# Two column parts of 64 in the sums and results of an attention kernel, with transposes, rows and banks of a piece in another order

## The chip, the core and the metric

The kernel runs on one core of one Trainium2 chip. The metric is the time of one execution on the device in microseconds (us). Three runs of the kernel before took 1344.69, 1345.78 and 1349.05 us; the median, 1345.78, stands for it. The profile is of one more execution, which took 1344.1 us. Engines are named as in the profile: PE is TensorE (PEld its weight loads), DVE is VectorE, ACT is ScalarE, POOL is GpSimd, SP is SyncE.

## The reference

Three layers follow one another on 8 batches of 576 positions. The first is attention with exponential features, for 8 heads of 64 channels:

```
phi(x)  = concat(exp(p - m), exp(-(p - m))),  p = x @ w_phi (64 x 128),  m = max|p| over the row
kv, z   = phi(k)^T v,  sum of phi(k) over the positions
out     = phi(q) kv / (phi(q) z + 1e-6)
```

The second mixes each position with the one before it by `mu_k` and `mu_r`, and computes `sigmoid(xr @ w_r) * (relu(xk @ w_k)^2 @ w_v)` with a hidden size of 1024. The third computes `h = relu(x @ w_in)`, a convolution of three taps over the positions, and `(h * sigmoid(conv)) @ w_out`. All data is float32.

## The kernel before, in words

The attention is cut into 32 pieces: a batch and a pair of its heads. Pieces 0 to 5 go through `attention`, an older path that this change leaves as it is. From piece 6 (`SW`) on, `block(Pi)` does one piece and prepares the next two:

- `turn` (L478): transposes on TensorE. `px` is the normalised result `xn` of the piece before, which ScalarE copies into `xT`, the input of the second layer; `pt` are the centred query projections of the two heads, which ScalarE turns into the features `qf` (L510); `pr` holds the last 64 positions of both (L500, L504).
- `rows_last`, `rows4` (L424, L433): projections of keys (`pk`, of piece Pi + 2) and queries (`pq`, of piece Pi + 1) and of the last positions (`p1`, listed as `p`), through L422. VectorE takes the maximum and centres (L441, L442).
- `sums4` (L466): `pkv`, the products of key features with values, of piece Pi + 1. Each product has 128 columns and is cut into column parts of 32, which write 32 partitions each (L474).
- `results` (L513): `pn`, the query features times `kvf`, of piece Pi, cut in the same way (L522); VectorE divides (L524 to L530).
- `features` (L451): ScalarE's exponentials for the keys of piece Pi + 2.

A float32 matmul in the program is two on the chip, so a product of four parts is eight matmuls and eight weight loads. The profile counts those of the chip.

The second layer ("expert work", `psk`, `psr`, `psv` through `mm3`, L143 to L145) is a generator `m`. `feed` takes steps from it between the blocks, so TensorE does a block, then 84 to 192 expert matmuls, then the next block. From piece 6 on TensorE's order is that of the program (`manual_schedule`); the order of the other engines is set by a scheduler that simulates the program. After the last piece (847 us) the rest of the second layer and the whole third layer follow, without attention beside them.

PSUM has eight banks. Three belong to the pool `psm` (tag "mm"), which the expert work uses too, and five to `psa` (tag "at"). Each pool hands its banks out in turn. A block takes three of "mm" and ten of "at", so a tile waits for the readers of the tile that had its bank three, or five, tiles earlier.

`bridge` (L535) stands between the two paths. It prepares piece 7 and then calls `run_late` (L368), which brings the last result of the older path into `xT`: two matmuls `pr` (L361) that need `rr`, four small rows that a DMA writes (L349).

Of the kernel before, what the change touches and what calls it, by code (L numbers as in the profile page):

```python
# [45 lines left out]
def fused_kernel(ctx: ExitStack, tc: tile.TileContext, qk, va, wphi, ones2, mu, wk, wv, wr, win, wout, cw, out):  # L46
# [103 lines left out]
    with ExitStack() as p1:  # L150
# [217 lines left out]
        def run_late():  # L368
            for l_ in late:
                l_()  # L370
            late.clear()
# [50 lines left out]
                T.matmul(o, x[r, j * P:j * P + P], wp0[r, h * FT:h * FT + FT], start=True, stop=True)  # L422

        def rows_last(Pi):  # L424
            ps = [psm.tile([P, 512], F32, tag="mm", name="p1"), psa.tile([P, 512], F32, tag="at", name="p1")]
            ps = [p_[:, :FT].rearrange("p (a n) -> p a n", a=1) for p_ in ps]
            rows(Pi, [(ps[h][:, 0], h, 4) for h in range(2)])
            t = pool.tile([P, 1, 2, FT], F32, tag="t1", bufs=2, name="t")
            for h in range(2):
                centre(ps[h], t[:, :, h])  # L430
            ts[Pi] = [t]

        def rows4(Pi, j0, nm):  # L433
            ps = [psa.tile([P, 4, FT], F32, tag="at", name=nm) for _ in range(2)]
            rows(Pi, [(ps[h][:, j], h, j0 + j) for j in range(4) for h in range(2)])
            return ps

# [28 lines left out]
        def sums4(Pi):  # L466

            kp, vt = kps_.pop(Pi), vts.pop(Pi)
            pkv = psa.tile([P, 2, 2, V1], F32, tag="at", name="pkv")
            prods = [(pkv[:, c, h], kp[h][:, i, c], vt[:, i, h]) for i in range(4) for h in range(2) for c in range(2)]  # L470
            prods += [(pkv[:, c], kp[2][:, c], vt[:, 4]) for c in range(2)]
            for i, (o, k_, v_) in enumerate(prods):
                for r in range(0, P, 32):
                    T.matmul(o[r:r + 32], k_[:, r:r + 32], v_, start=(i == 0), stop=(i == len(prods) - 1))  # L474
            kvs[Pi] = pool.tile([P, 2, 2, V1], F32, tag="kvh", bufs=2, name="kvf")
            A.copy(kvs[Pi], pkv)

        def turn(Pi):  # L478

            t1, *tq = ts[Pi]  # L480
            qf = [pool.tile([P, 2, S], F32, tag=("qh", "ql")[h], bufs=1, name="qf") for h in range(2)]
            if Pi - 1 in xns:
                xn = xns.pop(Pi - 1)
                px = psa.tile([P, 512], F32, tag="at", name="px")
                for j in range(4):
                    T.transpose(px[:, j * P:j * P + P], xn[:, j], ident)
            else:
                xn = None
            pr = psa.tile([P, 512], F32, tag="at", name="pr")
            if xn is not None:  # L490
                T.transpose(pr[:, :P], xn[:, 4], ident)
            for h in range(2):
                T.transpose(pr[:, P + h * P:2 * P + h * P], t1[:, 0, h], ident)
            if xn is not None:
                xt = main.tile([P, 2 + S], F32, tag="xT", bufs=XT, name="xT")
                G.memset(xt[:, 0:1], 0.0)
                A.copy(xt[:, 1:513], px)
                for h in range(2):
                    r = slice(64 * h, 64 * h + 64)
                    A.copy(xt[r, 513:577], pr[r, r])  # L500
                xT[divmod(Pi - 1, NP)] = xt
            for h in range(2):
                for c in range(2):
                    A.activation(qf[h][:, c, 512:], pr[:, P + h * P:P + h * P + 64], AF.Exp, scale=1.0 - 2 * c)  # L504
            for h in range(2):
                pt = psm.tile([P, 512], F32, tag="mm", name="pt")
                for j in range(4):
                    T.transpose(pt[:, j * P:j * P + P], tq[j // 2][:, j % 2, h] if Pi == SW else tq[h][:, j], ident)
                for c in range(2):
                    A.activation(qf[h][:, c, :512], pt, AF.Exp, scale=1.0 - 2 * c)  # L510
            return qf

        def results(Pi, qf):  # L513

            kv = kvs.pop(Pi)
            pn = [psa.tile([P, 512], F32, tag="at", name="pn")[:, :n * V1].rearrange("p (a n) -> p a n", n=V1) for n in (5, 4)]
            prods = [(0, 0, j, c) for j in range(4) for c in range(2)] + [(0, None, 4, c) for c in range(2)]
            prods += [(1, 1, j, c) for j in range(4) for c in range(2)]
            for b_, h, j, c in prods:
                for r in range(4):  # L520
                    h_, o = (r // 2, 512 + 32 * (r % 2)) if h is None else (h, j * P + 32 * r)
                    T.matmul(pn[b_][32 * r:32 * r + 32, j], qf[h_][:, c, o:o + 32], kv[:, c, h_], start=(j == 0 and c == 0), stop=(j == 4 - b_ and c == 1))  # L522
            rd = pool.tile([P, 9], F32, tag="rd4", bufs=2, name="rd")
            V.tensor_scalar(rd[:, :5], pn[0][:, :, D], 1e-6, None, ALU.add)  # L524
            V.tensor_scalar(rd[:, 5:], pn[1][:, :, D], 1e-6, None, ALU.add)
            V.reciprocal(rd, rd)
            xn = xns[Pi] = pool.tile([P, 5, P], F32, tag="xn", bufs=1, name="xn")
            for h in range(2):
                V.tensor_tensor(xn[:, :4, D * h:D * h + D], pn[h][:, :4, :D], rd[:, 5 * h:5 * h + 4].unsqueeze(2).to_broadcast([P, 4, D]), ALU.mult)
            V.tensor_scalar(xn[:, 4].rearrange("p (a n) -> p a n", a=2), pn[0][:, 4:5, :D].to_broadcast([P, 2, D]), rd[:, 4:5], None, ALU.mult)  # L530
            del ts[Pi]
# [3 lines left out]
        def bridge():  # L535

            rows_last(SW + 1)
            yield
            tk = centre4(rows4(SW + 1, 5, "pk"), "tk")
            load(SW + 2)  # L540
            yield
            features(SW + 1, tk)
            load_v(SW + 1)
            yield
            run_late()
            yield

        def block(Pi):

            nq, nk = Pi + 1 < B * NP, Pi + 2 < B * NP  # L550
            qf = turn(Pi)
            if nk:
                rows_last(Pi + 2)
                tk = centre4(rows4(Pi + 2, 5, "pk"), "tk")
            if nq:
                ts[Pi + 1] += centre4(rows4(Pi + 1, 0, "pq"), "tq")
                del xk[Pi + 1]
                sums4(Pi + 1)
            results(Pi, qf)
            if nk:  # L560
                features(Pi + 2, tk)
                load_v(Pi + 2)
            if Pi + 3 < B * NP:
                load(Pi + 3)

        def attention4(Pi):

            for n in range(NS):
                if n == 0:
                    while done[0] * NP <= Pi - 1 - XT:  # L570
                        next(m)
                    block(Pi)
                yield

        def mix(u, j):
# [280 lines left out]
```

## Time and profile before

| | |
|---|---|
| median of three runs | 1345.78 us |
| profiled execution, its span | 1344.1 us, 1342.3 us |
| TensorE busy | 1252.3 us (93%), 16,092 matmuls, as many weight loads |
| VectorE, ScalarE busy | 760.5 us (57%), 707.6 us (53%) |
| mean granted clock of TensorE | 0.985 of 2.4 GHz |
| pieces 6 to 31 | from 124 to 832 us |

In the 40 slices of the page TensorE shows 8 or 9 tenths busy up to about 800 us and 9 from there on. Its matmuls are pipelined: a row of the timeline gives the start of the first and the length up to the end of the last, and single matmuls in it overlap. A wait in brackets at the end of a row is the idle time before it and what ended it; "issue" means that nothing was waited for that the profile shows.

### The profile page before, as it was taken

To read this page: it belongs to the slowest core of one execution; us is meant where nothing else is said; L and a number is where in the kernel's file an instruction comes from. 1 tells how busy PE (TensorE), PEld (TensorE's weight loads), DVE (VectorE), ACT (ScalarE), POOL (GpSimd) and SP (SyncE) were. 2 spreads that over 40 slices of the span, in tenths; PEclk is the share of its full clock that TensorE was granted. 3 is DMA by queue.
4 is the path that set the end of the run, shared out by engine and by line. 5 is a ranking of instruction groups with operands and counts; after the bars stand their busy time and mean duration, and the time that the engine had idled before them with its cause. 6 is when DMAs were issued, how large, how long until landed. Compare 5 with 4: busy or idle time off the path is not lost.

```text
span 1342.3 us, 37269 instructions
## 1 busy us (share of the span) xinstructions
PE 1252.3 (93%) x16092; PEld 1216.9 (91%) x16092; DVE 760.5 (57%) x1457; ACT 707.6 (53%) x1654; POOL 137.7 (10%) x230
## 2 busy tenths in 40 slices
PE   8898899988898889898889999999999999999998
PEld 6687888988898889898888899999999999999998
DVE  7869654556556575465754553442754744744743
ACT  6877553545545455365553453442654654654653
POOL 6616300100001010010100000000000000000000
PEclk9998999989999999999999999999999999999999
DMA  7324212123222232222311100305012102112010
GB/s 252 108 57 131 92 34 64 53 83 100 70 79 85 69 103 81 79 85 70 100 59 47 38 21 20 144 19 179 24 49 72 36 37 71 33 39 71 26 46 36
DMA packets 56372, 96.13 MB, mean 72 GB/s; under 512 B 9100, under 2 KB 33808, under 8 KB 56208
## 3 DMA queue, kind: packets, MB, share of 16 engines
q1 hardware_dynamic: 42832, 65.89, 14.9%
q0 software_dynamic: 4528, 18.29, 4.5%
q10 hardware_dynamic: 8848, 9.57, 2.5%
q8 instruction: 126, 2.06, 0.6%
q14 instruction: 38, 0.31, 0.1%
HBM read 66.39 MB, written 27.26 MB: 70 GB/s over the span
## 4 chain that ended last, share of the span: by engine, by line
PE 85%; issue 6%; ACT 3%; DVE 3%; DMA 2%; POOL 1%; SPq 0%; DVEq 0%; ACTq 0%; POOLq 0%
PE psv L143 5%; PE psv L144 5%; PE psk L143 5%; PE psv L145 5%; PE psh L143 5%; PE psh L144 5%; PE pso L144 5%; PE pso L145 5%; PE psh L145 5%; PE pso L143 5%; PE psk L145 5%; PE psk L144 5%; PE pn L522 5%; PE pkv L474 4%; PE psr L143 2%
## 5 line engine op out<-in xcount | busy, mean ns | idle before, releaser
L143 PE MATMUL psv<-kh,wvl 128*128 128x288 f32 x512 | 154.3, 302 | 1.6 <-issue 1.6
L144 PE MATMUL psv<-kl,wvh 128*128 128x288 f32 x512 | 153.4, 300 | 1.7 <-issue 1.7
L143 PE MATMUL psk<-mh,wkl 128*128 128x288 f32 x512 | 154.9, 303 | 0.0
L145 PE MATMUL psk<-mh,wkh 128*128 128x288 f32 x512 | 152.3, 298 | 1.0 <-issue 1.0
L145 PE MATMUL psv<-kh,wvh 128*128 128x288 f32 x512 | 153.1, 299 | 0.1
L144 PE MATMUL psk<-ml,wkh 128*128 128x288 f32 x512 | 152.6, 298 | 0.0
L144 PE MATMUL psh<-xl,wih 128*128 128x288 f32 x512 | 151.1, 296 | 0.0
L143 PE MATMUL psh<-xh,wil 128*128 128x288 f32 x512 | 150.6, 296 | 0.0
L145 PE MATMUL psh<-xh,wih 128*128 128x288 f32 x512 | 150.1, 294 | 0.0
L626 ACT ACTIVATE kf<-psk 128x288 f32<-128x288 f32 x128 | 52.4, 410 | 184.7 <-PE psk L145 184.3
L144 PE MATMUL pso<-gl,woh 128*128 128x288 f32 x512 | 148.8, 295 | 0.0
L145 PE MATMUL pso<-gh,woh 128*128 128x288 f32 x512 | 148.7, 295 | 0.0
L143 PE MATMUL pso<-gh,wol 128*128 128x288 f32 x512 | 144.1, 293 | 0.0
L522 PE MATMUL pn<-kvf,qf 128*32 128x65 f32 x3744 | 70.4, 229 | 49.2 <-issue 47.4
L522 PEld LDWEIGHTS pn<-kvf,qf 128*32 128x32 f32 x3744 | 63.5, 114 | 54.2 <-issue 52.5
L760 DVE SCALAR_TENSOR_TENSOR ct<-h,cw,ct 128x576 f32<-128x576 f32 x64 | 52.4, 819 | 101.7 <-ACT ct L759 101.4
L143 PEld LDWEIGHTS psv<-kh,wvl 128*128 128x128 f32 x512 | 98.7, 193 | 3.2 <-issue 2.4
L144 PEld LDWEIGHTS psv<-kl,wvh 128*128 128x128 f32 x512 | 98.6, 193 | 1.9 <-issue 1.9
L143 PEld LDWEIGHTS psk<-mh,wkl 128*128 128x128 f32 x512 | 97.4, 191 | 2.8 <-issue 1.7
L69 POOL TENSOR_SCALAR hc<-hc 128x256 f32<-128x256 f32 (+1 forms) x53 | 60.1, 1137 | 379.8 <-ACT hc L68 301.0
L145 PEld LDWEIGHTS psv<-kh,wvh 128*128 128x128 f32 x512 | 98.5, 192 | 0.3 <-issue 0.3
L145 PEld LDWEIGHTS psk<-mh,wkh 128*128 128x128 f32 x512 | 97.9, 191 | 0.1
(145 smaller groups left out, 3159.6 us busy)
## 6 DMA issues: line engine op xcount, KB each, us to landing
rqk<-qk POOLq DMA_DIRECT2D x31, 576.0 KB, 4.5
va<-va SPq DMA_DIRECT2D x32, 325.0 KB, 4.2
x2s<-x SPq DMA_DIRECT2D x32, 288.0 KB, 2.3
x2r<-x2s ACTq DMA_DIRECT2D x32, 288.0 KB, 3.6
out<-ot SPq DMA_DIRECT2D x32, 288.0 KB, 2.1
raw<-wk SPq DMA_DIRECT2D x8, 512.0 KB, 5.7
raw<-wv SPq DMA_DIRECT2D x16, 256.0 KB, 2.7
raww<-win SPq DMA_DIRECT2D x16, 256.0 KB, 2.9
```

Of the source, the lines that this page charges most:

```text
L69: G.tensor_scalar(h, h, 2.0 ** -31, 122879.9921875 * 2.0 ** -16, ALU.max, ALU.min)
L143: T.matmul(ps, wl, xh, start=first, stop=False)
L144: T.matmul(ps, wh, xl, start=False, stop=False)
L145: T.matmul(ps, wh, xh, start=False, stop=last)
L474: T.matmul(o[r:r + 32], k_[:, r:r + 32], v_, start=(i == 0), stop=(i == len(prods) - 1))
L522: T.matmul(pn[b_][32 * r:32 * r + 32, j], qf[h_][:, c, o:o + 32], kv[:, c, h_], start=(j == 0 and c == 0), stop=(j == 4 - b_ and c == 1))
L626: A.activation(kf[:, j], ps, AF.Relu)
L760: V.scalar_tensor_tensor(t, h[:, 1:S + 1], cw0[:, fc, 1:2], t, ALU.mult, ALU.add)
```

## The change

`sums4` and `results` cut a product into two column parts of 64 where it was four of 32. `turn` transposes in the order `px`, `pt`, `pr` and takes `pt` from `psa`; ScalarE's copies out of `pr` come last. Both tiles of `rows_last` come from `psm`, and so does the second query tile of `rows4`. `run_late` leaves `bridge` and is called in `attention4` after the ninth of 15 steps of a piece (it has work in piece 6 alone).

```diff
@@ -422,7 +422,7 @@
                 T.matmul(o, x[r, j * P:j * P + P], wp0[r, h * FT:h * FT + FT], start=True, stop=True)
 
         def rows_last(Pi):
-            ps = [psm.tile([P, 512], F32, tag="mm", name="p1"), psa.tile([P, 512], F32, tag="at", name="p1")]
+            ps = [psm.tile([P, 512], F32, tag="mm", name="p1") for _ in range(2)]
             ps = [p_[:, :FT].rearrange("p (a n) -> p a n", a=1) for p_ in ps]
             rows(Pi, [(ps[h][:, 0], h, 4) for h in range(2)])
             t = pool.tile([P, 1, 2, FT], F32, tag="t1", bufs=2, name="t")
@@ -431,7 +431,8 @@
             ts[Pi] = [t]
 
         def rows4(Pi, j0, nm):
-            ps = [psa.tile([P, 4, FT], F32, tag="at", name=nm) for _ in range(2)]
+            ps = [psa.tile([P, 4, FT], F32, tag="at", name=nm)]
+            ps.append(psm.tile([P, 4, FT], F32, tag="mm", name=nm) if nm == "pq" else psa.tile([P, 4, FT], F32, tag="at", name=nm))
             rows(Pi, [(ps[h][:, j], h, j0 + j) for j in range(4) for h in range(2)])
             return ps
 
@@ -470,8 +471,8 @@
             prods = [(pkv[:, c, h], kp[h][:, i, c], vt[:, i, h]) for i in range(4) for h in range(2) for c in range(2)]
             prods += [(pkv[:, c], kp[2][:, c], vt[:, 4]) for c in range(2)]
             for i, (o, k_, v_) in enumerate(prods):
-                for r in range(0, P, 32):
-                    T.matmul(o[r:r + 32], k_[:, r:r + 32], v_, start=(i == 0), stop=(i == len(prods) - 1))
+                for r in range(0, P, 64):
+                    T.matmul(o[r:r + 64], k_[:, r:r + 64], v_, start=(i == 0), stop=(i == len(prods) - 1))
             kvs[Pi] = pool.tile([P, 2, 2, V1], F32, tag="kvh", bufs=2, name="kvf")
             A.copy(kvs[Pi], pkv)
 
@@ -479,35 +480,34 @@
 
             t1, *tq = ts[Pi]
             qf = [pool.tile([P, 2, S], F32, tag=("qh", "ql")[h], bufs=1, name="qf") for h in range(2)]
-            if Pi - 1 in xns:
+            old = Pi - 1 in xns
+            if old:
                 xn = xns.pop(Pi - 1)
+                xt = main.tile([P, 2 + S], F32, tag="xT", bufs=XT, name="xT")
+                xT[divmod(Pi - 1, NP)] = xt
+                G.memset(xt[:, 0:1], 0.0)
                 px = psa.tile([P, 512], F32, tag="at", name="px")
                 for j in range(4):
                     T.transpose(px[:, j * P:j * P + P], xn[:, j], ident)
-            else:
-                xn = None
-            pr = psa.tile([P, 512], F32, tag="at", name="pr")
-            if xn is not None:
-                T.transpose(pr[:, :P], xn[:, 4], ident)
-            for h in range(2):
-                T.transpose(pr[:, P + h * P:2 * P + h * P], t1[:, 0, h], ident)
-            if xn is not None:
-                xt = main.tile([P, 2 + S], F32, tag="xT", bufs=XT, name="xT")
-                G.memset(xt[:, 0:1], 0.0)
                 A.copy(xt[:, 1:513], px)
-                for h in range(2):
-                    r = slice(64 * h, 64 * h + 64)
-                    A.copy(xt[r, 513:577], pr[r, r])
-                xT[divmod(Pi - 1, NP)] = xt
-            for h in range(2):
-                for c in range(2):
-                    A.activation(qf[h][:, c, 512:], pr[:, P + h * P:P + h * P + 64], AF.Exp, scale=1.0 - 2 * c)
-            for h in range(2):
-                pt = psm.tile([P, 512], F32, tag="mm", name="pt")
+            for h in range(2):
+                pt = psa.tile([P, 512], F32, tag="at", name="pt")
                 for j in range(4):
                     T.transpose(pt[:, j * P:j * P + P], tq[j // 2][:, j % 2, h] if Pi == SW else tq[h][:, j], ident)
                 for c in range(2):
                     A.activation(qf[h][:, c, :512], pt, AF.Exp, scale=1.0 - 2 * c)
+            pr = psa.tile([P, 512], F32, tag="at", name="pr")
+            if old:
+                T.transpose(pr[:, :P], xn[:, 4], ident)
+            for h in range(2):
+                T.transpose(pr[:, P + h * P:2 * P + h * P], t1[:, 0, h], ident)
+            for h in range(2):
+                for c in range(2):
+                    A.activation(qf[h][:, c, 512:], pr[:, P + h * P:P + h * P + 64], AF.Exp, scale=1.0 - 2 * c)
+            if old:
+                for h in range(2):
+                    r = slice(64 * h, 64 * h + 64)
+                    A.copy(xt[r, 513:577], pr[r, r])
             return qf
 
         def results(Pi, qf):
@@ -517,9 +517,9 @@
             prods = [(0, 0, j, c) for j in range(4) for c in range(2)] + [(0, None, 4, c) for c in range(2)]
             prods += [(1, 1, j, c) for j in range(4) for c in range(2)]
             for b_, h, j, c in prods:
-                for r in range(4):
-                    h_, o = (r // 2, 512 + 32 * (r % 2)) if h is None else (h, j * P + 32 * r)
-                    T.matmul(pn[b_][32 * r:32 * r + 32, j], qf[h_][:, c, o:o + 32], kv[:, c, h_], start=(j == 0 and c == 0), stop=(j == 4 - b_ and c == 1))
+                for r in range(2):
+                    h_, o = (r, 512) if h is None else (h, j * P + 64 * r)
+                    T.matmul(pn[b_][64 * r:64 * r + 64, j], qf[h_][:, c, o:o + 64], kv[:, c, h_], start=(j == 0 and c == 0), stop=(j == 4 - b_ and c == 1))
             rd = pool.tile([P, 9], F32, tag="rd4", bufs=2, name="rd")
             V.tensor_scalar(rd[:, :5], pn[0][:, :, D], 1e-6, None, ALU.add)
             V.tensor_scalar(rd[:, 5:], pn[1][:, :, D], 1e-6, None, ALU.add)
@@ -541,9 +541,6 @@
             yield
             features(SW + 1, tk)
             load_v(SW + 1)
-            yield
-            run_late()
-            yield
 
         def block(Pi):
 
@@ -570,6 +567,8 @@
                     while done[0] * NP <= Pi - 1 - XT:
                         next(m)
                     block(Pi)
+                if n == 8:
+                    run_late()
                 yield
 
         def mix(u, j):
```

What follows is the order of instructions on an engine. TensorE in a block, before: `px`, `pt` and `pr` are transposes, `p` the rows of the last positions, `pk` and `pq` key and query rows, `pkv` sums, `pn` results.

```order
L486 MATMUL px<-ident,xn 128x128 x4
L491 MATMUL pr<-ident,xn 128x128
L493 MATMUL pr<-ident,t 128x128 x2
L508 MATMUL pt<-ident,t 128x128 x8
L422 MATMUL p_1961<-wp_74,rqk 128x128
L422 MATMUL p_1962<-wp_74,rqk 128x128
L422 MATMUL pk<-wp_74,rqk 128x128 x8
L422 MATMUL pq<-wp_74,rqk 128x128 x8
L474 MATMUL pkv<-va,kp 32x65 x64
L474 MATMUL pkv<-va,kr 32x130 x8
L522 MATMUL pn<-kvf,qf 32x65 x72
```

The same block on TensorE, now:

```order
L491 MATMUL px<-ident,xn 128x128 x4
L496 MATMUL pt<-ident,t 128x128 x8
L501 MATMUL pr<-ident,xn 128x128
L503 MATMUL pr<-ident,t 128x128 x2
L422 MATMUL p_1889<-wp_74,rqk 128x128
L422 MATMUL p_1890<-wp_74,rqk 128x128
L422 MATMUL pk<-wp_74,rqk 128x128 x8
L422 MATMUL pq<-wp_74,rqk 128x128 x8
L475 MATMUL pkv<-va,kp 64x65 x32
L475 MATMUL pkv<-va,kr 64x130 x4
L522 MATMUL pn<-kvf,qf 64x65 x36
```

The small transposes moved behind the large ones, and sums and results have half as many matmuls.

ScalarE at the start of a block that follows expert products `psk`, before (`whl` is a weight in preparation, `kf` the eviction of an expert product):

```order
L497 COPY xT<-px 128x512
L500 COPY xT<-pr 64x64 x2
L504 ACTIVATE qf<-pr 128x64 x3
L124 CAST whl<-hc 128x256
L626 ACTIVATE kf<-psk 128x288
L504 ACTIVATE qf<-pr 128x64
L510 ACTIVATE qf<-pt 128x512 x4
```

The same place on ScalarE, now:

```order
L492 COPY xT<-px 128x512
L498 ACTIVATE qf<-pt 128x512 x2
L124 CAST whl<-hc 128x256
L625 ACTIVATE kf<-psk 128x288
L498 ACTIVATE qf<-pt 128x512 x2
L506 ACTIVATE qf<-pr 128x64 x4
L510 COPY xT<-pr 64x64 x2
```

The eviction stands behind one copy and two large exponentials where it stood behind three copies and three small ones; all that reads `pr` moved to the end.

TensorE from the bridge into block 6, before (the rows ahead are expert matmuls):

```order
L145 MATMUL psr<-mh_968,wrh 128x288
L361 MATMUL pr<-rr,on_81 128x288 x2
L493 MATMUL pr<-ident,t 128x128 x2
L508 MATMUL pt<-ident,t 128x128 x8
L422 MATMUL p_1473<-wp_74,rqk 128x128
L422 MATMUL p_1474<-wp_74,rqk 128x128
```

The same place on TensorE, now:

```order
L145 MATMUL psk<-mh_952,wkh 128x288
L503 MATMUL pr<-ident,t 128x128
L422 MATMUL p_1445<-wp_74,rqk 128x128
L422 MATMUL p_1446<-wp_74,rqk 128x128
L422 MATMUL pk<-wp_74,rqk 128x128 x8
```

The transposes `pt` and one of `pr` now stand ahead of the last 12 matmuls of `psk`. The 12 matmuls of `psr` and the two of L361 left this place: the former follow block 6, the latter stand 48 expert matmuls after it, between two products `psv`.

## Rows read from the trace of the kernel before

**Rows 1.** The page, chain that ended last: share of the span by engine

```profile
PE 85%; issue 6%; ACT 3%; DVE 3%; DMA 2%; POOL 1%; SPq 0%; DVEq 0%; ACTq 0%; POOLq 0%
```

**Rows 2.** Waits of TensorE, 125 to 835: us in total, times, longest

```profile
PE pn L522 <- issue: 47.4, 26, 3.5
PE p L422 <- ACT kf L626: 6.9, 8, 0.9
PE pkv L474 <- issue: 6.1, 5, 3.1
PE psv L144 <- issue: 1.7, 1, 1.7
PE psv L143 <- issue: 1.6, 1, 1.6
PE p L422 <- DVE x L657: 1.5, 1, 1.5
```

**Rows 3.** Timeline of TensorE, a block at 437: start, us, instruction, [idle before]

```profile
437.35 0.60 PE L486 MATMUL px<-ident,xn 128*128 128x128 f32 x4
...
441.28 2.03 PE L474 MATMUL pkv<-va,kp 128*32 128x65 f32 x128
443.13 0.63 PE L474 MATMUL pkv<-va,kr 128*32 128x130 f32 x16
443.58 0.41 PE L522 MATMUL pn<-kvf,qf 128*32 128x65 f32 x16
446.57 2.03 PE L522 MATMUL pn<-kvf,qf 128*32 128x65 f32 x128 [2.59 <-issue]
```

**Rows 4.** The page: TensorE's instructions, and the queue of instruction packets

```profile
PE 1252.3 (93%) x16092; PEld 1216.9 (91%) x16092; DVE 760.5 (57%) x1457; ACT 707.6 (53%) x1654; POOL 137.7 (10%) x230
...
q8 instruction: 126, 2.06, 0.6%
```

**Rows 5.** DMA queues, 430.7 to 452.2: packets, MB, share

```profile
q8 instruction: 3, 0.05, 0.9%
```

**Rows 6.** DMA queues, 444.1 to 452.2

```profile
q8 instruction: 3, 0.05, 2.3%
```

**Rows 7.** Busy time by stretch: length, PE, PEld, DVE, ACT, POOL, clock, DMA, GB/s

```profile
430.70:443.80 13.10, 13.10 (x263) 12.81 (x262) 8.79 (x22) 7.53 (x21) 1.89 (x2) 1.00 0.33 93
```

**Rows 8.** Groups of instructions, TensorE, 125 to 835: busy, mean ns, idle before

```profile
L522 PE MATMUL pn<-kvf,qf 128*32 128x65 f32 x3744 | 70.4, 229 | 49.2 <-issue 47.4 <-ACT qf L510 1.1 <-DVE t L442 0.7
...
L474 PE MATMUL pkv<-va,kp 128*32 128x65 f32 x3200 | 51.6, 220 | 2.1 <-issue 1.7 <-PE pq L422 0.4
```

**Rows 9.** Timeline of TensorE, sums with full 128-column loads

```profile
82.15 0.78 PE L279 MATMUL pkv<-va,kp 128*128 128x65 f32 x6
```

**Rows 10.** The same, first and last of nine stretches at half clock

```profile
185.50:188.70 3.20, 3.20 (x26) 3.02 (x16) 1.39 (x5) 0.00 (x0) 0.00 (x0) 0.50 0.02 5
...
755.60:758.80 3.20, 3.20 (x55) 3.02 (x47) 1.39 (x5) 0.00 (x0) 0.00 (x0) 0.50 0.02 5
```

**Rows 11.** The same, a stretch of the later expert work

```profile
1000.00:1100.00 100.00, 100.00 (x757) 100.00 (x756) 53.45 (x71) 53.36 (x101) 1.52 (x15) 1.00 0.15 48
```

**Rows 12.** Timeline of TensorE, expert matmuls at half clock

```profile
419.41 0.44 PE L145 MATMUL psk<-mh,wkh 128*128 128x288 f32 x1
419.65 0.44 PE L143 MATMUL psk<-mh,wkl 128*128 128x288 f32 x1
```

**Rows 13.** Timeline of ScalarE, eviction and exponentials of a block at 405

```profile
407.36 0.43 ACT L626 ACTIVATE kf<-psk 128x288 f32<-128x288 f32 x1
...
407.77 2.10 ACT L510 ACTIVATE qf<-pt 128x512 f32<-128x512 f32 x4
```

**Rows 14.** Timeline of ScalarE and TensorE around block 6

```profile
122.76 0.62 ACT L456 ACTIVATE kp<-t 128x512 f32<-128x512 f32 x1
...
123.63 0.82 PE L361 MATMUL pr<-rr,on 128*128 128x288 f32 x2 [5.30 <-DMA rr<-r]
...
134.33 1.00 PE L522 MATMUL pn<-kvf,qf 128*32 128x65 f32 x55 [0.65 <-issue]
```

More of the change, by code (lines that the diff above doesn't have):

```diff
@@ L486, in turn @@
                     T.transpose(px[:, j * P:j * P + P], xn[:, j], ident)
-            else:
-                xn = None
-            pr = psa.tile([P, 512], F32, tag="at", name="pr")
-            if xn is not None:
-                T.transpose(pr[:, :P], xn[:, 4], ident)
-            for h in range(2):
-                T.transpose(pr[:, P + h * P:2 * P + h * P], t1[:, 0, h], ident)
-            if xn is not None:
-                xt = main.tile([P, 2 + S], F32, tag="xT", bufs=XT, name="xT")
-                G.memset(xt[:, 0:1], 0.0)
-                A.copy(xt[:, 1:513], px)
-                for h in range(2):
-                    r = slice(64 * h, 64 * h + 64)
-                    A.copy(xt[r, 513:577], pr[r, r])
-                xT[divmod(Pi - 1, NP)] = xt
-            for h in range(2):
-                for c in range(2):
-                    A.activation(qf[h][:, c, 512:], pr[:, P + h * P:P + h * P + 64], AF.Exp, scale=1.0 - 2 * c)
-            for h in range(2):
-                pt = psm.tile([P, 512], F32, tag="mm", name="pt")
+                A.copy(xt[:, 1:513], px)
+            for h in range(2):
+                pt = psa.tile([P, 512], F32, tag="at", name="pt")
                 for j in range(4):
```

## The prediction

> **What bounds the kernel now.** I read the chain that ended last first: 85% of the span is TensorE at work, and the next largest share is 6% "issue", some 80 us in which TensorE waited for nothing that the profile names [rows 1]. So the path runs through TensorE from end to end, and time that is taken from TensorE comes off the end. Next I read TensorE's waits over the stage of the blocks, 125 to 835 us. "Issue" heads them: 47.4 us in 26 waits before a result matmul (L522), 6.1 in 5 before a sum, 1.7 and 1.6 in two waits at expert matmuls; what stands behind is 6.9 us for ScalarE (L626) and 1.5 us for VectorE (L657) before the first row matmul of a block [rows 2]. That makes 56.8 us of issue and 8.4 us of named waits.
>
> The timeline of one block says where the issue time lies [rows 3]. The block starts at 437.35, and up to 443.58 every group follows the one before without a gap. Sixteen result matmuls later TensorE stops for 2.59 us, runs 128 of them, and stops again before the first expert matmul, the 1.6 us of [rows 2]. Between there is no operand to wait for: the same tiles were used just before.
>
> What came in the stop is an instruction packet. The page lists 126 packets of instructions with 2.06 MB on one queue [rows 4], that is 16.4 KB each; 2 x 16,092 TensorE instructions in 126 packets are 255 each. From 430.7 to 452.2 there were three such packets, and all three lie between 444.1 and 452.2 [rows 5, 6]. So none came from 430.7 until TensorE stopped at 443.8. In that time, up to 443.58 + 0.41 less the length of the last matmul, it issued 263 matmuls and 262 weight loads, 525 instructions [rows 7], two packets' worth. It had used up what it held. The two stops end 3.6 us apart, at 446.57 and at about 450.2 (446.57 + 2.03 + 1.6), and between them TensorE ran about one packet's worth. I read this as the pace of the queue: 256 / 3.6 = 71 instructions per us.
>
> Sums and results need more than that. 128 sum matmuls span 2.03 us, the last of them 0.22 [rows 3]: (2.03 - 0.22) / 31.75 = 0.057 us per set of four column parts, with eight instructions in it, 140 per us. One block has 144 + 144 such matmuls, 576 instructions in some 4.5 us, behind 102 more of transposes and rows. This is twice what the queue brings, so TensorE empties its store in nearly every one of the 25 blocks that have both.
>
> **The change, part by part.** The sum is made against the profiled execution, 1344.1 us, 1.7 below the median of the three runs.
>
> Two column parts instead of four. Each product of 64 columns does the work of two, so the 7,344 matmuls of L522 and L474 (3,744, 3,200 [rows 8], and 16 with 130 columns in each of 25 blocks [rows 3]) become 3,672, each with its load. A block falls from 678 to 390 instructions, its sums and results from 576 to 288. If a set keeps its length these take 4.6 us, 63 instructions per us, below the 71 that the queue brings, and with two packets held at the start the store does not run empty. I take all issue waits as gone: -56.8 us. Each of these waits hides a little more: it is counted from the listed end of a matmul, while the next one would have started 0.2 us before that end; 33 waits by 0.2 is -6.6 us.
>
> The length of a set is the unknown. Four parts together pass 65 columns in 0.057 us. The 16 matmuls with 130 columns span 0.63 us [rows 3]; less one length (0.275) and the offset inside a set (0.02) this is 0.112 per set for twice the columns. So the time goes with the columns that stream, and loads cost nothing at four parts. With full 128-column loads six matmuls of 65 columns span 0.78 us, the last one 0.26 [rows 9]: 0.103 each, which is the load showing. Half of that, for 64 columns, is 0.052, just under the 0.057 of the stream, as long as the two parts load side by side. I take 0.059 per set. There are 7,344 / 4 = 1,836 sets: +3.7 us. Bounds: 0.054 (the stream alone) gives -5.5; load and stream one after the other, 0.052 + 0.057, gives +95.
>
> On this point the page TensorE: Matmul & The Clock Gate of the Trainium skill, section "Part 3: Packing small matmuls", speaks against the change: a load overlaps a running matmul only where the two use different row groups, and here all parts use all rows. By that rule load and stream would always add up, and the time would be that of rival two. The trace disagrees at four parts, since 0.057 leaves no room for a load; whether it holds at two parts no row shows, and it is the slow rival below.
>
> The clock. Nine stretches between 185 and 759 us show a granted clock of 0.5, that is 1.2 GHz, 32.2 us together [rows 10], and each follows one of the longer stops. Expert matmuls there start 0.24 us apart (419.41, 419.65 [rows 12]), while 757 in 100 us make 0.132 at the full clock [rows 11]. If TensorE no longer stops, 32.2 x (1 - 0.132 / 0.24) = 14.5 us come back, less what lies inside the stops themselves: -13. Between 0 (the clock falls for other reasons) and -14.5.
>
> Transposes and banks. In the kernel before every second block waits before its first row matmul, because one bank of the rows is that of the last expert product, and its eviction (L626) stands in ScalarE's order behind copies and exponentials [rows 13]. In the change the rows take the two older banks, and the newest goes to the second query bank, about 3.0 us after the block's start. ScalarE then does one copy, two exponentials, a cast and that eviction, which by the durations of before ends about 2.9 us after the start. That is -8.4 us. New waits take their place: the first sum needs the second transpose bank, whose exponentials (0.52 us each [rows 13]) end about 3.85 us after the start where TensorE wants it at 3.95. Both margins are 0.1 us. I charge 0.2 per block, +5; between 0 and +23 (0.93 in each of 25 blocks, a whole wait of the kind that goes). Behind the first sum all sums and results queue on TensorE, and nothing else does. The later read of the small bank is covered: it ends some 4.9 us after the start and its next user is the first result at 6.3.
>
> The late pieces. TensorE stands 5.3 us for a small DMA at 123.63 [rows 14]. Moved nine steps back, that work finds its data long there, and TensorE goes straight to block 6. Late next is ScalarE: the features of piece 7 end at 123.4 [rows 14], and sums and results (4.6 us) follow, so the block ends near 128.1 instead of 135.3 [rows 14], with 12 expert matmuls and two small ones (2.2 us) still to do. -5 us; 0 if the weights that are made in this stretch are then late, -7 at best.
>
> Sum: -56.8 - 6.6 + 3.7 - 13 - 8.4 + 5 - 5 = -81.1, or 1263. From 847 us on the same expert work follows back to back, so nothing there gives the gain back.
>
> **The rivals.** One: something else takes part of the place of the stops: the two margins of 0.1 us are missed by a whole eviction in every block (+18 beyond what I charge), or a set takes 0.07 us (+20). For it: VectorE and ScalarE are the two that blocks wait for already [rows 2], and the gain leaves them less time per block. Against: at the sums the kernel before shows no wait for ScalarE [rows 2]. 1280 to 1300.
>
> Two, slower: with only two parts the next load of a part is not covered by the others' matmuls, and a set takes load plus stream, 0.109. For it: at 128 columns the load shows [rows 9], and this change doubles the load of a part. Against: in that row a matmul costs 0.103, and not 0.103 + 0.057, so a load does run beside a matmul of the same rows. Price 1,836 x 0.052 = 95 instead of 3.7: 1354, slower. It decides from (81.1 + 3.7) / 1,836 = 0.046 more per set, 0.103 us.
>
> Three: the stops are not a matter of how many instructions are asked for, and halving them doesn't do what it should. Then only waits and late pieces move: 1344.1 - 8.4 - 5 + 5 + 3.7 = 1339. Against it: no packet in 13 us, then the stop at the second packet's worth, then a packet. The page Runtime: NRT & Kernel Launch of the Trainium skill, section "Instruction fetch mechanics", would have it so: TensorE holds 2,048 instructions in blocks of 256 and the refill is mostly hidden. Blocks of 255 agree with the trace; a store of 2,048 does not, for TensorE stopped after 525 without a refill.
>
> **How the numbers follow.** Forecast 0.70 (own range 1248 to 1280), rival one 0.15, two 0.08, three 0.07. I predict 1263. The range takes in the forecast and rival one, 1246 to 1302; what is left out is two, three and the edges. A measurement of this kernel tells about 0.3% (4 us) from no change: faster by more 0.88 (forecast, one, most of three), within 0.05 (parts of two and three), slower 0.07.
>
> **What would show it.** Right: TensorE's issue waits in the stage under 10 us where they were 57; some 30 instruction packets fewer; a set of two parts starting every 0.057 to 0.062 us; a full clock from 185 us to the end; the last block's results some 80 us earlier. Wrong: sets at 0.1 us or more (rival two); issue waits that stay while packets fall (three); or new waits for L498 or L625 before the sums and the query rows, or for VectorE (one).

## The result, and the profile after

The changed kernel takes 1258.65 us (median of four runs, 1256.33 to 1259.02), the kernel before 1347.12 (four runs, 1344.69 to 1349.05): ratio 0.934, 95% interval 0.9319 to 0.9362. Its profiled execution took 1258.99 us, with a span of 1257.1 (before 1342.3: 85.2 less) and a mean granted clock of 0.996 (before 0.985).

Of the page: engines' busy time, the queue of instruction packets, and the chain that ended last by engine, to be laid beside [rows 1, 4]:

```profile
PE 1236.5 (98%) x12420; PEld 1208.9 (96%) x12420; DVE 759.1 (60%) x1457; ACT 707.2 (56%) x1654; POOL 139.6 (11%) x230
...
q8 instruction: 98, 1.61, 0.5%
...
PE 88%; DVE 4%; ACT 3%; issue 2%; DMA 1%; POOL 1%; SPq 0%; DVEq 0%; ACTq 0%; POOLq 0%
```

TensorE's busy time is only 15.8 us less, with 3,672 matmuls fewer. What went is TensorE's idle time: its busy share rose from 93 to 98%. There are 28 packets fewer, and "issue" fell from 6% of the chain to 2%. Now TensorE's waits, 125 to 835 us, all that the view lists (us in total, times, longest), against [rows 2]:

```profile
PE pk L422 <- ACT xT L492: 1.5, 2, 1.3
PE pn L522 <- ACT qf L498: 0.2, 1, 0.2
```

No wait for issue is left, and none for L625, which is the L626 of before. A block in the timeline of TensorE (start, us, instruction), against [rows 3]; it follows `psk`, so it is one of those that waited for an eviction before:

```profile
420.25 0.60 PE L491 MATMUL px<-ident,xn 128*128 128x128 f32 x4
420.68 1.04 PE L496 MATMUL pt<-ident,t 128*128 128x128 f32 x8
421.56 0.27 PE L501 MATMUL pr<-ident,xn 128*128 128x128 f32 x1
421.67 0.38 PE L503 MATMUL pr<-ident,t 128*128 128x128 f32 x2
421.98 0.49 PE L422 MATMUL p<-wp,rqk 64*128 64x128 f32 x4
422.30 1.06 PE L422 MATMUL pk<-wp,rqk 64*128 64x128 f32 x16
423.20 1.26 PE L422 MATMUL pq<-wp,rqk 64*128 64x128 f32 x16
424.39 2.09 PE L475 MATMUL pkv<-va,kp 128*64 128x65 f32 x64
426.30 0.61 PE L475 MATMUL pkv<-va,kr 128*64 128x130 f32 x8
426.75 2.27 PE L522 MATMUL pn<-kvf,qf 128*64 128x65 f32 x72
```

No row has a bracket. The 64 sum matmuls are 32 sets of two parts; less the last matmul's 0.22 us they give (2.09 - 0.22) / 31.5 = 0.059 us per set, and the 72 results (2.27 - 0.22) / 35.5 = 0.058. Before it was 0.057 [rows 3]. From `px` to the next expert matmul a block takes 8.50 us in 13 of the 25 blocks from piece 7 on, and 8.70 in eight, which all follow `psk`. Of the other four, piece 7 takes 12.26, one at 667 us takes 9.24, and the last two have less to do. Before it was 9.8 to 13.6 in the full blocks. All 25 together make 283.6 us before and 214.1 now, 69.5 less. The expert stretches between them came down from 413.4 to 400.2, and up to piece 7 it is 2.5 us. That is the whole of the 85.2: the last result goes into `px` at 761.5 us, where it was 846.7, and from there both kernels take 495.6.

The stretches at half clock, and the rest of the stage (columns as in [rows 7]; the clock is the last but two), against [rows 10]:

```profile
121.90:128.70 6.80, 6.30 (x86) 6.08 (x88) 6.80 (x13) 4.82 (x15) 4.09 (x6) 0.50 0.50 144
152.60:156.00 3.40, 3.40 (x52) 3.18 (x50) 3.21 (x8) 1.72 (x9) 1.16 (x3) 0.50 0.10 23
160.00:760.00 600.00, 599.44 (x7528) 589.96 (x7527) 374.73 (x840) 338.65 (x874) 52.70 (x78) 1.00 0.24 75
```

From 160 to 760 us TensorE is idle for 0.56 us (before, in the same stretch, for 61.3) and holds the full clock. The nine stretches of before have gone; a short one at 152 is new. The one at 121.9 is not: the kernel before has a stretch of the same 6.8 us at 120.6.

### The profile page after: what moved, and what is told of

It is laid out like the page before. It is cut to its first block, busy times and chain, and to the rows that moved or that the text cites. A ratio compares the mean times of both kernels' runs of the same rounds, so it can differ in the third digit from the quotient of the medians.

```text
span 1257.1 us, 29948 instructions
## 1 busy us (share of the span) xinstructions
PE 1236.5 (98%) x12420; PEld 1208.9 (96%) x12420; DVE 759.1 (60%) x1457; ACT 707.2 (56%) x1654; POOL 139.6 (11%) x230
## 3 DMA queue, kind: packets, MB, share of 16 engines
q1 hardware_dynamic: 42832, 65.89, 15.8%
## 4 chain that ended last, share of the span: by engine, by line
PE 88%; DVE 4%; ACT 3%; issue 2%; DMA 1%; POOL 1%; SPq 0%; DVEq 0%; ACTq 0%; POOLq 0%
PE psh L143 5%; PE psh L144 5%; PE pso L144 5%; PE pso L145 5%; PE psh L145 5%; PE pso L143 5%; PE psv L143 5%; PE psk L143 5%; PE psv L144 5%; PE psv L145 5%; PE psk L145 5%; PE pkv L475 5%; PE psk L144 5%; PE pn L522 4%; PE psr L143 3%; PE psr L145 3%
## 5 line engine op out<-in xcount | busy, mean ns | idle before, releaser
L143 PE MATMUL psv<-kh,wvl 128*128 128x288 f32 x512 | 151.5, 296 | 0.0
L625 ACT ACTIVATE kf<-psk 128x288 f32<-128x288 f32 x128 | 52.3, 409 | 120.6 <-PE psk L145 120.2
L627 DVE TENSOR_TENSOR kf<-kf 128x576 f32<-128x576 f32 x64 | 48.4, 756 | 79.9 <-ACT kf L625 79.7
L145 PEld LDWEIGHTS psh<-xh,wih 128*128 128x128 f32 x512 | 96.2, 188 | 0.0
```

Of the source, the lines that this page charges most:

```text
L143: T.matmul(ps, wl, xh, start=first, stop=False)
L145: T.matmul(ps, wh, xh, start=False, stop=last)
L625: A.activation(kf[:, j], ps, AF.Relu)
L627: V.tensor_tensor(kf, kf, kf, ALU.mult)
```

## The experiments

Each ratio and each gain is against the kernel before as it ran beside the experiment: 1347.44 us for the first four kernels, 1346.55 for the next three, 1348.80 for the last three.

### The two column parts alone

The kernel before with both loops of 64, its order and banks untouched:

```diff
-                for r in range(0, P, 32):
-                    T.matmul(o[r:r + 32], k_[:, r:r + 32], v_, ...
+                for r in range(0, P, 64):
+                    T.matmul(o[r:r + 64], k_[:, r:r + 64], v_, ...
...
-                for r in range(4):
-                    h_, o = (r // 2, 512 + 32 * (r % 2)) if h is None else (h, j * P + 32 * r)
+                for r in range(2):
+                    h_, o = (r, 512) if h is None else (h, j * P + 64 * r)
...
```

> The kernel before with two column parts of 64 in sums and results, and nothing else of the change. Theory (the stops come from instruction packets that arrive at about 70 instructions per us while sums and results ask for 140): issue waits of TensorE in the stage of the blocks fall from 57 us to under 5, instruction packets from 126 to about 98, the clock stays full after 190 us; the waits for the eviction before the rows (8.4 us) and the stop at the bridge (5.3 us) stay, so the time is the changed kernel's 1258.7 plus 8 plus 3: 1266 to 1274. Rival (the new order of transposes, rows and banks took the stops away, and the parts little): over half of the issue waits stay, 1310 or more.

Measured: 1268.16 us (1266.34 to 1268.33), ratio 0.9412 [0.9386, 0.9437]; 98 packets. TensorE's waits, 125 to 835 us:

```profile
PE p L422 <- ACT kf L626: 6.9, 8, 0.9
PE pr L361 <- ACT kp L456: 5.2, 1, 5.2
PE p L422 <- DVE x L657: 2.2, 1, 2.2
```

and two rows of a block after `psk` in its timeline:

```profile
427.59 0.49 PE L422 MATMUL p<-wp,rqk 64*128 64x128 f32 x4 [0.87 <-ACT kf L626]
...
428.81 1.06 PE L422 MATMUL pq<-wp,rqk 64*128 64x128 f32 x16
```

All issue waits are gone, while the waits for evictions stand as before. So the parts alone do that, and bring 79 of the 88 us. Blocks take 8.50 us, and 9.43 where the row of L626 stands.

### The order alone

The changed kernel with four parts of 32 in both loops:

```diff
-                for r in range(0, P, 64):
-                    T.matmul(o[r:r + 64], k_[:, r:r + 64], v_, ...
+                for r in range(0, P, 32):
+                    T.matmul(o[r:r + 32], k_[:, r:r + 32], v_, ...
...
-                for r in range(2):
+                for r in range(4):
...
```

> The changed kernel with four column parts of 32 again; order, banks and the late call stay as changed. Theory: 126 packets, issue waits of 50 to 60 us and the half clock stay; only the waits for the eviction (8.4 us) and half of the stop at the bridge (2.5 us) go, 1332 to 1340. Rival (order and banks took the stops away): under 1300.

Measured: 1339.95 us (1336.45 to 1343.15, seven runs), ratio 0.9942 [0.9915, 0.9968]; 126 packets. The first and the third of TensorE's waits:

```profile
PE pn L522 <- issue: 53.0, 27, 3.2
...
PE psk L143 <- issue: 2.4, 1, 2.4
```

The new order takes the eviction waits of 6.9 us away and leaves the stops: the waits for issue are 63.8 us in all, where I expected 50 to 60. It gives 7.5 us. The two halves sum to 79.3 + 7.5 = 86.8, against 88.5 for both together: within what these medians tell, they add up.

### The late pieces back in the bridge

The changed kernel with `run_late` where it was:

```diff
             load_v(SW + 1)
+            yield
+            run_late()
+            yield
...
-                if n == 8:
-                    run_late()
                 yield
```

> The changed kernel with the late piece called in the bridge again, ahead of block 6. Theory: TensorE stands about 5 us for the small DMA again and the clock falls there, but the next blocks then find weights and mixes ready, so that 2 to 4 us of it show at the end: 1261 to 1263. Rival (the weights and ScalarE set the pace up to block 7, so the move gave nothing): 1258.7 within 1.

Measured: 1258.32 us (1257.66 to 1260.55), ratio 0.9345 [0.9323, 0.9368], the same as the changed kernel. Two rows of TensorE's timeline, the late work and the start of piece 7:

```profile
123.22 0.51 PE L361 MATMUL pr<-rr,on 128*128 128x288 f32 x2 [3.83 <-DMA rr<-r]
...
147.55 0.60 PE L491 MATMUL px<-ident,xn 128*128 128x128 f32 x4
```

The wait for the small DMA is back with 3.8 us, and piece 7 starts 0.3 us later than in the changed kernel (147.22, below). But block 6 no longer waits for ScalarE and block 7 hardly does (0.5 us), and block 7 ends at 157.7 us, where it ends at 159.5 in the changed kernel. So the move gave nothing: I expected 2 to 4 us from it, and the rival held.

### The same instructions, spread

The kernel before, its four parts kept, with 24 expert matmuls between sums and results:

```diff
                 sums4(Pi + 1)
+            for _ in range(2):
+                credit[0] -= 1
+                next(m, None)
             results(Pi, qf)
```

> The kernel before with four column parts, the same number of instructions and the same order of transposes and banks; but two of the expert steps (24 matmuls, 48 instructions in 3.2 us) that follow a block stand between its sums and its results. Theory (pace of the packets): the packets have 3.2 us to catch up in the middle of the burst; with packets every 3.7 to 4.0 us the issue waits fall from 57 us to between 6 and 13, most of the half clock goes with them, packets stay 126, and the time is 1284 to 1294. Rival (stops belong to matmuls of four parts as such, or to the number of instructions of a block): issue waits stay above 45 us, 1335 or more.

Measured: 1286.58 us (1284.49 to 1291.15), ratio 0.9557 [0.9529, 0.9585]; 126 packets and 16,092 matmuls, as before. TensorE's waits, 125 to 835 us, without those of the bridge:

```profile
PE p L422 <- ACT kf L629: 6.9, 8, 0.9
PE pn L522 <- issue: 6.2, 9, 1.5
...
PE pkv L474 <- issue: 4.3, 4, 2.7
```

Not one instruction less, and still four fifths of the stops go: from 56.8 us of the four kinds that the prediction summed to 11.4 (6.2 + 4.3 + 0.9 at `psv`). The matmuls between are slow (24 x 0.132 = 3.2 us for 48 instructions), which gives the packets time to come in. What counts is how fast instructions are used up over a few us, not how many there are.

### One part of four and one of two; and the same number at a slower pace

Two kernels with 534 TensorE instructions per block, between the 390 of the changed kernel and the 678 of before. The first is the changed kernel with four parts in the results alone; the second keeps two parts and issues the products of the results twice (the second pass starts the accumulation anew; it adds nothing to the first). The edits, one after the other:

```diff
-                for r in range(2):
-                    h_, o = (r, 512) if h is None else (h, j * P + 64 * r)
+                for r in range(4):
+                    h_, o = (r // 2, 512 + 32 * (r % 2)) if h is None else (h, j * P + 32 * r)
...
```

```diff
-            for b_, h, j, c in prods:
+            for b_, h, j, c in prods + prods:
```

> The changed kernel with four parts of 32 in the results alone (sums stay at two of 64). A block then asks for 534 instructions in some 8.5 us. Theory (pace of the packets, one per 3.7 to 4.0 us): 112 packets, issue waits of 10 to 19 us where the kernel before had 57 and the changed one none, and with what the waits hide and a little of the half clock 1272 to 1290. Rival (stops go with the number of four-part matmuls, of which half remain): 25 to 32 us of issue waits, 1295 to 1310.

> The changed kernel, whose results are multiplied twice over in every block (the second pass adds the same products again before the division, so that the output is scaled in both numerator and denominator). A block asks for 534 instructions as in the run with four-part results, but in 10.6 us. Theory (the pace of 62 instructions per us in sums and results is below that of the packets): 112 packets, issue waits under 3 us, and 936 more sets of 0.058 us: 1313 within 5. Rival (the store is what counts: a block of more than two packets' worth, 512, makes TensorE stop): 10 us of issue waits or more, 1325 or more.

Measured: four parts in the results, 1281.26 us (1278.48 to 1285.18), ratio 0.9535 [0.9486, 0.9583]; twice, 1316.29 (1314.45 to 1318.2), 0.9794 [0.9738, 0.9851]. Both have 112 packets. The waits for issue before L522, first of the four parts:

```profile
PE pn L522 <- issue: 11.5, 9, 3.3
```

then of the products issued twice, with a block's row of results:

```profile
PE pn L522 <- issue: 2.9, 3, 1.8
```

```profile
454.31 4.37 PE L522 MATMUL pn<-kvf,qf 128*64 128x65 f32 x144
```

288 instructions in (4.37 - 0.22) us are 69 per us, just under the 71 that the prediction read off the queue; most blocks run without a stop. The same 288 at up to 140 per us stop nine times, for 3.0 to 3.3 us in the three longest. (The second kernel is slower for its doubled work, 2.1 us in each block; its stops are what counts here.)

### One part of 128

The changed kernel without column parts, in the results too (only the last positions of the two heads, 64 each, stay two matmuls):

```diff
-                for r in range(0, P, 64):
-                    T.matmul(o[r:r + 64], k_[:, r:r + 64], v_, ...
+                for r in range(0, P, P):
+                    T.matmul(o[r:r + P], k_[:, r:r + P], v_, ...
...
```

> The changed kernel with one part of 128 columns in sums and results (the last 64 positions keep their two parts of 64). Theory (a load takes 0.8 ns per column, beside the stream, and parts load side by side): the load now bounds a set, 0.107 to 0.112 us instead of 0.058 in 1,732 of 1,836 sets, no issue waits, about 84 packets, 1258.7 + 86 to 93: 1340 to 1355. Rival (load and stream one after the other as soon as parts don't cover it): 0.16 us, 1435.

Measured: 1345.97 us (1342.69 to 1352.73, ten runs), ratio 1.0015 [0.9987, 1.0043]. There are 84 packets and no issue wait. Its sums in TensorE's timeline:

```profile
461.00 3.79 PE L475 MATMUL pkv<-va,kp 128*128 128x65 f32 x32
464.62 0.66 PE L475 MATMUL pkv<-va,kr 128*128 128x130 f32 x4
```

A product of 65 columns takes (3.79 - 0.275) / 31 = 0.113 us, the length of a matmul there being 0.275; twice that of two parts. The four products of 130 columns behind them start at 464.62, 464.79, 464.90 and 465.01, and the first result at 465.12: after the first step 0.112 apart, the same for twice the stream. So at 65 columns the load sets the pace. It stands in place of the stream and not, as rival two had it, on top of it: load and stream in turn would have taken longer for 130 columns than for 65. A full block takes 12.08 us in place of 8.50, which eats up the whole gain with no stop in sight.

### Expert work ahead of block 6

The late pieces had brought nothing, and TensorE waits in block 6. The two kernels pull two and four expert steps (24 and 48 matmuls) ahead of its rows, at the end of `bridge`; the changed kernel ran beside them once more:

```diff
             load_v(SW + 1)
+            for _ in range(2):      # 4 in the other
+                credit[0] -= 1
+                next(m, None)
```

> The changed kernel once more, unaltered, beside the two that follow. Both theories: 1257 to 1260 us, waits of about 1.3 us for ScalarE at the key rows and 1.2 us at the query rows of block 6, and half clock from 122 to 129 us.

> The changed kernel with two steps of the expert work (24 matmuls, 3.2 us at 0.132 each) taken from behind block 6 and put ahead of its rows. Theory (TensorE loses 2.5 us to ScalarE at the rows of block 6 and some 3 us to the half clock that follows, and work that waits for nothing can stand in their place): the two waits of block 6 go, the half clock after them too, 2 to 5 us less than the unaltered kernel, 1254 to 1257. Rival (ScalarE sets the pace up to block 7, so a wait that is filled comes back at block 7): within 1.5 us of the unaltered kernel, and the waits of block 7 grow by what those of block 6 lose.

> The same with four steps (48 matmuls, 6.3 us). Theory: no waits in block 6, as with two steps or 1 us better, if block 7 waits less as well: 1253 to 1257. Rival: within 1.5 us of the unaltered kernel; the block starts later by 6 us and with it ScalarE's exponentials for piece 7.

Measured: unaltered 1258.99 us (1256.67 to 1260.2); two steps 1259.4 (1257.11 to 1261.32), four 1260.68 (1259.37 to 1261.97). Against before that is 0.9327 [0.9299, 0.9354], 0.9334 [0.9303, 0.9364] and 0.9342 [0.9316, 0.9369]: nothing gained, if anything a little lost with four. TensorE's waits from 110 to 160 us, unaltered:

```profile
PE pk L422 <- ACT xT L492: 1.3, 1, 1.3
PE pk L422 <- ACT qf L498: 1.2, 1, 1.2
PE pq L422 <- ACT kf L625: 1.2, 1, 1.2
```

two steps:

```profile
PE p L422 <- ACT sg L646: 2.2, 2, 1.2
PE pk L422 <- ACT xT L492: 1.8, 1, 1.8
PE p L422 <- ACT kf L628: 1.0, 1, 1.0
```

and the first two of four steps:

```profile
PE pq L422 <- DVE x L659: 1.5, 1, 1.5
PE pk L422 <- ACT xT L492: 1.3, 1, 1.3
```

The waits that were filled come back under other names, for ScalarE (L646, L628, L492) and VectorE (L659). By the timelines block 6 waits 2.3 us unaltered, 2.2 with two steps and 1.1 with four, and block 7 waits 1.4, 2.9 and 3.3. The half clock moves with them: with four steps it has left block 6, and 6.8 us of it stand in block 7. The theory fell. The rival held, but for four steps, which are 1.7 us above the unaltered kernel where it allowed 1.5.

## Why the prediction was right, and where it was not

**What bounds the kernel.** Right. The stops were TensorE's want of instructions: they went when sums and results asked for half as many (parts alone), and for the most part when the same number was spread or was used at 69 per us. Rival three, that the stops have another cause, is out. I expected some 30 packets fewer, and there are 28. The pace of 71 per us stood well enough for 69 to be nearly free of stops and 140 not. It can be had without the two stops, too: the three packets of [rows 6] start at 444.14, 447.66 and 451.20 us, 3.5 apart, and between 150 and 835 us no two packets of the kernel before start less than 3.3 us apart. A packet itself takes 1.0 us; what makes up the rest no run shows. The refill that the page Runtime: NRT & Kernel Launch of the Trainium skill (section "Instruction fetch mechanics") calls mostly hidden was not hidden here: 56.8 us before, 53.0 before L522 alone with the new order and four parts.

**Stops, what they hide, sets and clock.** The four terms came to -56.8 - 6.6 + 3.7 - 13 = -72.7. The parts alone measured -79.3 by the medians, and -75.9 by the profiled spans (1342.3 and 1266.4), which is the side that the sum was made on. The stops went entirely, as charged. A set measured 0.058 to 0.059 where I took 0.059, so that term is about +2.5 and not +3.7. The nine stretches at half clock are gone. That leaves 2 us by the spans and 5 by the medians that came back beyond what I had counted; which of stops, hidden parts and clock holds them the runs did not separate.

The length of a set settles rival two. In the block at 420 sets of 130 columns start 0.111 us apart, so 65 columns stream in about 0.056, and 0.058 to 0.059 leaves no room for a load: it is hidden at two parts as well. The rule that a load overlaps only where the row groups differ (the Trainium skill, TensorE: Matmul & The Clock Gate, "Part 3: Packing small matmuls") does not hold here at two parts, as it did not at four. But it was closer than I wrote. I had misread the row of full loads [rows 9]: 0.103 was the mean of five steps, of which the first is 0.057 and the other four are 0.112, the pace that the kernel without parts shows. If a load goes with its columns, one of 64 takes half of that, 0.056, an estimate, and two side by side lie just under the stream. One step further the load decides.

**Evictions and new waits.** Right in what goes; of the two margins one held and one was just missed. ScalarE in the block at 420 (start, us, instruction), against [rows 13]:

```profile
420.88 0.59 ACT L492 COPY xT<-px 128x512 f32<-128x512 f32 x1
421.37 1.09 ACT L498 ACTIVATE qf<-pt 128x512 f32<-128x512 f32 x2
...
422.63 0.43 ACT L625 ACTIVATE kf<-psk 128x288 f32<-128x288 f32 x1
422.93 1.11 ACT L498 ACTIVATE qf<-pt 128x512 f32<-128x512 f32 x2
```

The eviction ends at 423.06, 2.81 us after the block's start, where I had 2.9 and TensorE wants its bank at 3.0. The exponentials end at 424.04, 3.79 after it (I had 3.85), and the first sum comes at 4.14: that margin held. The new wait is not in front of the sums, where I put it, but in the query rows: `pq` spans 1.26 us in the block at 420, against 1.06 in the kernel with the parts alone. Its first matmul starts at 423.20 and the second, into the bank that L625 sets free, at 423.33, where the two start 0.01 us apart in a block after `psv`. That is 0.27 us after the eviction's end, a lag for which I had left no room; no wait listed names it. The new wait costs 0.2 us in eight blocks. The block at 667 loses 0.7, and there the wait listed is the key rows' for ScalarE's copy (L492, 0.2 us). Together this is some 2.3 us, where I charged 5.

**The late pieces.** Here the step failed: -5 was charged for taking the wait of 5.3 us [rows 14] out of the bridge, and it is worth 0 (the kernel with `run_late` put back runs as fast). TensorE's timeline from block 6 on in the changed kernel shows what is in its place:

```profile
119.79 1.23 PE L422 MATMUL pk<-wp,rqk 64*128 64x128 f32 x15 [1.35 <-ACT qf L498]
...
122.40 2.07 PE L422 MATMUL pq<-wp,rqk 64*128 64x128 f32 x14 [1.15 <-ACT kf L625]
124.40 3.73 PE L475 MATMUL pkv<-va,kp 128*64 128x65 f32 x64
...
137.41 0.43 PE L361 MATMUL pr<-rr,on 128*128 128x288 f32 x2
147.22 0.60 PE L491 MATMUL px<-ident,xn 128*128 128x128 f32 x4
...
150.97 1.16 PE L422 MATMUL pk<-wp,rqk 64*128 64x128 f32 x14 [1.30 <-ACT xT L492]
```

L361 itself waits for nothing now, as forecast. But the rows of block 6 wait for ScalarE, 1.35 and 1.15 us, the clock falls to a half at 121.9 us, and the sums take 3.73 us instead of 2.09. In block 7 the rows wait again, 1.30 us, and the half clock returns. With `run_late` back in the bridge these waits shrink to 0.5 us, and the half clock there to 3.4 us from 6.8. So the step that failed is that TensorE, freed of the DMA, would go straight through block 6: I had the sums at 123.4 us and the block's end at 128.1, and they came at 124.40 and 131.0. I named ScalarE as late next, but only for the sums and not for the rows. The bound of 0 came out, though not for its reason: no wait for weights is listed there. Filling these waits moved them, so more work for TensorE does not help there. What sets the pace was not isolated. The nearest row is that of the stretch from 100 to 152 us in the changed kernel:

```profile
100.00:152.00 52.00, 47.84 (x474) 45.05 (x472) 49.26 (x110) 37.28 (x97) 30.99 (x38) 0.93 0.40 119
```

VectorE is busy for 49.26 of 52 us, more than TensorE with 47.84. That makes it a candidate and no more: the kernel with `run_late` put back is as fast with VectorE busy for 45.61 us of the same stretch, and no run lightened it.

**The sum.** -81.1 was predicted and the profiled spans differ by 85.2. By these spans the parts alone give 75.9, 3.2 more than charged. The rest of the change gives 9.3 where -8.4 + 5 - 5 = -8.4 was charged: the new waits cost 2.7 less, 5 us for the late pieces did not come, and some 3 us are left that no run assigns. So errors of a few us cancelled, and that the total is off by 4 only is in part luck; the large terms were right in kind and in size. The time of 1258.65 lies in the likeliest case's own range. Of the signs that I named, no issue wait, 28 packets fewer, sets of 0.058 us, the full clock (from 156 us on) and a last result 85 us earlier all came; of the signs of being wrong a small one came too, the 0.2 us before the query rows.

## What to carry to other kernels

Where a matmul waits for "issue" and its operands are old, count the instructions that TensorE uses per us over the last few us, and look when the packets of the instruction queue came: a kernel may be starved of instructions with no engine late. Here larger column parts cured it, and slow matmuls put between the fast ones took away four fifths. But a part's load must still hide behind the streaming, and with full-width loads of products of 65 columns it doesn't. And a wait can move instead of going: the 5.3 us of the bridge came back as waits of the next two blocks for ScalarE, and filling those moved them again.

## What the runs showed of the hardware

- Two kernels with the same number of TensorE instructions in a block stop for 11.5 us and for 2.9 us: the burst at 140 per us stops, the one at 69 mostly not. In the kernel before TensorE used at most 544 instructions between the starts of two packets, and no two packets started less than 3.3 us apart (150 to 835 us).
- Column parts that use the same rows load side by side: a set of 65 columns takes 0.057 us in four parts, 0.058 to 0.059 in two, and 0.113 as one load of 128 columns. One load of 128 columns also runs beside the stream of the product before it: products of 130 columns start 0.112 us apart, as those of 65 do.
- From 160 to 760 us the half clock came with the stops: nine stretches with 56.8 us of stops (before), three, 13.7 us together, with 11.5 (four parts in the results alone), one of 3.4 us with 11.4 (the same instructions spread), none without any (after, and the parts alone). Each of the three stands at one of the three longest stops of its kernel, 3.0 to 3.3 us. In block 6 of the changed kernel two waits of 1.35 and 1.15 us stand just before and at the start of 6.8 us of it.
